# A fixed order for all four engines in the first expert layer of batch 0, and an earlier end of the weight decoding inside attention

## The chip, the cores and the metric

The kernel runs on one core of one Trainium2 chip. The metric is the device time of one execution in microseconds (us). A time of "before" or "after" is the median of three runs. TensorE is called PE, ScalarE ACT, VectorE DVE, GpSimd POOL, SyncE SP; SP only issues DMAs here.

## What is computed

Three layers follow each other. Clustered attention (2 batches, 8 heads, 768 tokens, head size 64) gives x; the first expert layer is a plain two-matrix network on 1536 tokens; a second layer routes each token to two of eight experts.

```python
attn_out = _attn_ref(q, k, v, centroids)            # softmax over keys of the same cluster
x = attn_out.transpose(0, 2, 1, 3).reshape(B * S, H * D)
h = x @ w_in                                        # 1536x512 @ 512x2048
g = h * (1.0 / (1.0 + np.exp(-1.702 * h)))
y = g @ w_out                                       # 1536x2048 @ 2048x512
return _moe2_ref(y, w_gate, w_noise, noise, w1, w2) # top 2 of 8 experts
```

All inputs are float64 or float32; `w_in` and `w_out` come as float64, as pairs of 32-bit words, and have to be turned into float32 on the chip.

## The kernel before

**Stages.** Attention handles one pair of heads of one batch at a time: 8 units (4 of batch 0, then 4 of batch 1) of 12 steps each. Its instructions stand in one list on each engine, sorted by the table `TIMES`, whose entries are in steps; 12 U = 96 is the step at which the last unit would end. The first expert layer then runs on batch 0 (`moe1(0)`) and on batch 1 (`moe1(1)`), and the second layer follows.

**The first expert layer.** The hidden size 2048 is cut into 16 blocks `fb` of 128. Every float32 operand is kept as two parts, a rounded high part and the rest (`wih`, `wil`, `woh`, `wol` for the weights, `xh`, `xl` for x, `gh`, `gl` for g), and a product takes three matmuls. `gemm1(fb)` gives two halves of 384 tokens, 12 matmuls of 384 columns each, in PSUM banks 0 and 1. Each half goes through ACT (`sg`, L736), DVE (`g`, L738), ACT (`gh`, L739) and DVE (`gl`, L740). `gemm2(fb)` adds 18 matmuls of 512 columns into the other six banks. On PE the order is gemm1(0), gemm1(1), gemm2(0), gemm1(2), gemm2(1) and so on; it is fixed by hand. The other engines' order in this layer is chosen by the scheduler at build time. Inside a half the matmuls go `wih*xh, wih*xl, wil*xh` for each quarter of the contraction, so `wil` is wanted by the third matmul.

**Decoding a weight tile.** `decode_part` turns a 128x512 tile of 64-bit words into float32: ACT takes the magnitude (L113) and the sign (L120), POOL clamps (L115), DVE shifts (L116) and ors in the low word (L118), POOL multiplies by the sign (L122). Then `split1` makes the high part on ACT (L717, called hi below) and the low part on POOL (L718, called lo). Each block has two tiles, `wi` and `wo`, so per block: ACT 4 + 2 instructions, POOL 2 clamps, 2 multiplications, 2 lo, DVE 2 shifts and 2 ors, besides sg, g, gh, gl for two halves. For batch 0 this is done for blocks 2 to 15 in the layer itself; blocks 0 and 1 are decoded inside attention, at the steps `w000` to `w114` of the table (block, tile, part). `moe1(1)` reuses the float32 tiles and only splits them.

**Transfers.** SP loads the 64-bit tiles, `si` and `so`, 512 KB each, into two buffers each (`b_stg`). That memory is part of what attention used, so the first of these loads can start only when attention's own tiles there have been read.

**End of attention.** After the last scores a chain of small steps remains for each group of columns: POOL copies (`rb`, L476), PE transposes (L484), DVE copies (L488), POOL adds (L465, L466), multiplies (L492), ACT writes `xh` (L498), POOL `xl` (L505). Their place in the lists is fixed by the table; how they mix with the expert layer's instructions on an engine is the scheduler's choice.

Of the kernel before, what the change touches and what calls it, by code (L numbers as in the profile page):

```python
# [8 lines left out]
F32 = mybir.dt.float32  # L9
# [12 lines left out]
NB = S // 128  # L22
# [22 lines left out]
WARM = (8, 8, 12)  # L45
TAIL = 3
NE = 2
DEC = 5
TIMES = {
# [10 lines left out]
    9.64, "P:xl3": 8.971, "P:xsk": 17.159, "P:xsq": 12.921, "P:ld": 6.496, "P:cc": 8.65, "P:cm0": 10.462,  # L60
    "P:cm1": 10.511, "P:cm2": 10.389, "P:cm3": 9.796, "P:co": 10.569, "P:ct": 11.969, "P:c1": 12.019, "P:ce":
    12.222, "P:cr": 13.092, "P:c2": 14.203, "P:ch": 14.578, "P:ht": 16.263, "P:ho": 22.149, "P:hs": 25.249,
# [6 lines left out]
    7.93, "L:oi": 0.369, "L:or": 7.324, "L:oa": 8.518, "L:ot": 9.79, "L:oc": 10.14, "L:om": 10.5, "L:oh": 11.6, "L:ol":  # L69
# [18 lines left out]
}  # L88
WVE = ()
ORDER = (0, 4, 1, 5, 2, 6, 3, 7)  # L90
# [12 lines left out]
def f(ap):  # L103
    return ap.bitcast(F32)


def decode_part(nc, src, t, dst, part):

    low = src.bitcast(U32).rearrange("p (n t) -> p n t", t=2)[:, :, 0]
    high = src.bitcast(F32).rearrange("p (n t) -> p n t", t=2)[:, :, 1]  # L110
    mag, sgn, bits = t[:, 0], t[:, 1], t[:, 2].bitcast(U32)
    if part == 0:
        nc.scalar.activation(mag, high, AF.Abs, scale=65536.0)  # L113
    elif part == 1:
        nc.gpsimd.tensor_scalar(mag, mag, BIG, TINY, op0=OP.min, op1=OP.max)  # L115
        nc.vector.tensor_scalar(bits, mag.bitcast(U32), 3, 0x7FFFFFFF, op0=OP.logical_shift_left, op1=OP.bitwise_and)  # L116
    elif part == 2:
        nc.vector.scalar_tensor_tensor(bits, low, 29, bits, op0=OP.logical_shift_right, op1=OP.bitwise_or)  # L118
    elif part == 3:
        nc.scalar.activation(sgn, high, AF.Sign)  # L120
    else:
        nc.gpsimd.tensor_mul(dst, f(bits), sgn)  # L122
# [483 lines left out]
class Moe:  # L606
# [87 lines left out]
        nc.sync.dma_start(wo, self.w_out[fb * 128:(fb + 1) * 128])  # L694
        self.st1[fb] = (wi.rearrange("p k f -> p (k f)"), wo)

    def decode(self, src, dst):
        t = self.dec.tile([128, 3, DM], F32, tag="dec", name="dec")
        for part in range(DEC):
            decode_part(self.nc, src, t, dst, part)  # L700

    def split1(self, b, fb):
        nc = self.nc
        if b == 0:
            if fb < NE:
                wi, wo = self.raw[2 * fb:2 * fb + 2]
            else:
                si, so = self.st1.pop(fb)
                wi, wo = (self.wA(F32, 2 * fb + i, f"w{'io'[i]}{fb}") for i in range(2))
                self.decode(si, wi)  # L710
                self.decode(so, wo)
            self.W1.append((wi, wo))
        out = []
        for nm, src in zip(("wi", "wo"), self.W1[fb]):
            hi = self.wr.tile([128, DM], F32R, tag=nm + "h", name=f"{nm}h{fb}")
            lo = self.wr.tile([128, DM], F32R, tag=nm + "l", name=f"{nm}l{fb}")
            nc.scalar.activation(hi, src, AF.Copy)  # L717
            (nc.vector if b else nc.gpsimd).tensor_sub(lo, src, f(hi))  # L718
            out += [hi, lo]
        v = lambda t: t.rearrange("p (k f) -> p k f", k=KB)  # L720
        return v(out[0]), v(out[1]), out[2], out[3]

    def gemm1(self, b, fb):
        nc = self.nc
# [666 lines left out]
@with_exitstack  # L1391
def kernel(ctx, tc, q, k, v, centroids, moe_w_in, moe_w_out,
                                                         w_gate, w_noise, noise, w1, w2, out):
    nc = tc.nc
    pool = lambda c, name, bufs, **kw: c.enter_context(tc.tile_pool(name=name, bufs=bufs, reuse_waits="tile", **kw))
    const = pool(ctx, "const", 1)
    x1 = pool(ctx, "x1", 1, side="right")
    dram = ctx.enter_context(tc.tile_pool(name="dram", bufs=1, space=bass.MemoryType.DRAM))
    xs = dram.tile([E * REG, ROW], F32, name="xs")
    tab = dram.tile([ROUNDS * E, 4], F32, name="tab")  # L1400
    ident = const.tile([128, 128], F32, name="ident")
    make_identity(nc, ident)
    identb = const.tile([128, 128], BF16, name="identb")
    nc.vector.tensor_copy(identb, ident)
    ab = pool(ctx, "a_ab", 1)
    x0ctx = ExitStack()
    x0 = pool(x0ctx, "x0", 1, side="right")
    xh = [p.tile([128, NP, S], F32R, tag=f"xh{b}", name=f"xh{b}") for b, p in enumerate((x0, x1))]
    xl = [p.tile([128, NP, S], F32R, tag=f"xl{b}", name=f"xl{b}") for b, p in enumerate((x0, x1))]
    moe = Moe(tc, const, (moe_w_in, moe_w_out, w_gate, w_noise, noise, w1, w2), ident, xh, xl, xs, tab, out)  # L1410
    moe.x1 = x1
    with ExitStack() as actx:
        a = Attention(tc, actx, const, ab, q, k, v, centroids, (moe_w_in, moe_w_out), ident, identb, xh, xl)
        a.hooks = {3 + 2 * i: [lambda i=i: moe.init_piece(i)] for i in range(44)}
        a.hooks[1] = [moe.consts]
        a.run()
    moe.ab, moe.raw, moe.wg = ab, a.raw, a.g("raw", 0)
    moe.open_all(ctx)
    bctx, b0ctx = ExitStack(), ExitStack()
    moe.open1(bctx, b0ctx)  # L1420
    with tc.high_priority(PRI):
        for fb in range(NE):
            moe.S[0, fb] = moe.split1(0, fb)
        for fb in range(NE, FB1):
            moe.load1(fb)
    with tc.manual_schedule(engines={mybir.EngineType.PE}):
        acc = moe.moe1(0)
    R0 = [moe.row(0, acc, j) for j in range(NB)]
    b0ctx.close()
    x0ctx.close()  # L1430
    moe.open2(ctx)
    s = {"W": []}
    run = moe.logits0(R0)

    def hook(fb):
        if fb % 2:
            s["W"] += moe.weights_part(0, 0, fb // 2, (w1[0], w2[0]))
        if 1 <= fb <= NB:
# [58 lines left out]
```

## Time and profile before

| | us |
|---|---|
| median of 3 runs (lowest, highest) | 949.79 (948.38, 954.39) |
| the profiled execution | 955.92 |
| its span, first to last instruction | 954.2 |
| PE busy in the span | 886.9 (93%) |
| DVE, ACT, POOL busy | 598.8, 491.8, 359.3 |
| mean granted clock of TensorE | 0.969 of 2.4 GHz |

How to read it: matmuls are pipelined, so the busy time of PE counts overlapping instructions once and doesn't mean that the array is at its peak. An instruction that waits for an engine's shared resource after it has started is counted as busy, so a long duration of a short instruction is itself a reading.

### The profile page before, as it was taken

The numbers are of one execution on the slowest core, as the hardware profiler recorded it, in microseconds if no ns is written. First come the engines' busy times: TensorE is split into PE (matmuls) and PEld (weight loads), VectorE is DVE, ScalarE is ACT, GpSimd is POOL, SyncE is SP. The second block draws the span as 40 slices with busy tenths as digits, with TensorE's granted clock in tenths as the row PEclk, the third lists the DMA queues.
The fourth block names the chain that finished last, engine by engine and source line by source line (L and its number), as shares of the span: only waits on it lengthen the run. The fifth ranks groups of instructions, "written<-read, shape, count | busy, mean of one in ns | idle before, by whom it ended". The sixth has DMA issues, their size and how long they took to land. (4 is left out here: it accounts for less than half of the span.)

```text
span 954.2 us, 14930 instructions
## 1 busy us (share of the span) xinstructions
PE 886.9 (93%) x5277; PEld 813.9 (85%) x5277; DVE 598.8 (63%) x1190; ACT 491.8 (52%) x1021; POOL 359.3 (38%) x398
## 2 busy tenths in 40 slices
PE   6999999999895999999999999979999899999993
PEld 4898989899784988888998979868889899999992
DVE  3889999999875667765447553835663446454231
ACT  2788888888875565555345433414443234332210
POOL 3134443444537776770000501462332233342121
PEclk8899999999998999999999999889999899999997
DMA  7756675676314334312100331264675646562120
GB/s 208 187 139 182 166 202 135 178 191 190 112 34 137 103 119 129 103 35 67 45 23 23 145 97 45 78 232 132 210 206 145 159 123 203 152 189 80 33 65 34
DMA packets 77532, 120.14 MB, mean 126 GB/s; under 512 B 9858, under 2 KB 55939, under 8 KB 76941
## 3 DMA queue, kind: packets, MB, share of 16 engines
q1 hardware_dynamic: 69997, 100.98, 36.9%
q0 software_dynamic: 7456, 18.16, 5.9%
q8 instruction: 43, 0.70, 0.3%
q14 instruction: 36, 0.29, 0.1%
HBM read 72.85 MB, written 23.76 MB: 101 GB/s over the span
## 5 line engine op out<-in xcount | busy, mean ns | idle before, releaser
L426 DVE TENSOR_TENSOR PTl<-ps_pt,PTh 128x384 fp32r<-128x384 f32 x192 | 98.7, 549 | 10.5 <-ACT PTh L421 9.5
L421 ACT ACTIVATE PTh<-ps_pt 128x384 fp32r<-128x384 f32 x192 | 87.6, 495 | 28.9 <-PE ps_pt L411 27.4
L733 PE MATMUL bank<-xh,wih 128*128 128x384 f32 x256 | 89.6, 350 | 11.6 <-ACT wih L717 6.3
L394 DVE TENSOR_REDUCE nm<-ps_s 128x1 f32<-128x768 f32 x96 | 91.2, 950 | 12.7 <-PE ps_s L389 12.3
L733 PE MATMUL bank<-xh,wil 128*128 128x384 f32 x256 | 89.1, 348 | 5.5 <-POOL wil L718 5.5
L411 PE MATMUL ps_pt<-ident,P 128*128 128x128 f32 x576 | 88.2, 277 | 3.9 <-DVE PTl L426 3.4
L402 ACT ACTIVATE P<-ps_s,nm 128x768 f32<-128x768 f32 x96 | 87.3, 910 | 4.7 <-DVE nm L394 4.5
L733 PE MATMUL bank<-xl,wih 128*128 128x384 f32 x256 | 87.9, 343 | 0.0
L1259 ACT ACTIVATE hh<-bank 128x240 fp32r<-128x240 f32 (+6 forms) x80 | 35.2, 446 | 99.8 <-PE bank L1251 83.5
L1251 PE MATMUL bank<-xT,wB 128*128 128x240 f32 (+3 forms) x480 | 83.0, 321 | 0.0
L411 PEld LDWEIGHTS ps_pt<-ident,P 128*128 128x128 f32 x576 | 68.3, 141 | 14.3 <-DVE PTl L426 11.5
L1251 PEld LDWEIGHTS bank<-xT,wB 128*128 128x128 f32 x480 | 77.9, 193 | 2.4
L1260 DVE SCALAR_TENSOR_TENSOR hl<-bank,hh 128x240 fp32r<-128x240 f32 (+6 forms) x80 | 40.3, 506 | 57.5 <-ACT hh L1259 56.8
L748 PE MATMUL bank<-woh,gh 128*128 128x512 f32 x192 | 76.3, 397 | 0.0
L748 PE MATMUL bank<-wol,gh 128*128 128x512 f32 x192 | 75.0, 391 | 0.0
L1056 POOL TENSOR_TENSOR wA<-stg,wA 128x512 fp32r<-128x512 f32 x16 | 20.7, 1294 | 142.8 <-DVE wol L718 69.8
L748 PE MATMUL bank<-woh,gl 128*128 128x512 f32 x192 | 70.8, 391 | 0.0
L388 PE MATMUL ps_s<-k,q 128*128 128x384 f32 x192 | 70.3, 366 | 0.2 <-ACT P L402 0.2
L389 PE MATMUL ps_s<-k,q 80*128 80x384 f32 x192 | 66.3, 345 | 2.7 <-DMA q<-ohT 2.7
L1289 POOL DMA_INDIRECT out_dram<-Y,idx x31 | 33.0, 1066 | 78.3 <-DVE Y L1288 68.5
L733 PEld LDWEIGHTS bank<-xh,wih 128*128 128x128 f32 x256 | 49.4, 193 | 14.3 <-ACT wih L717 6.7
L733 PEld LDWEIGHTS bank<-xh,wil 128*128 128x128 f32 x256 | 49.2, 192 | 9.6 <-POOL wil L718 9.5
(294 smaller groups left out, 2206.3 us busy)
## 6 DMA issues: line engine op xcount, KB each, us to landing
stg<-in_moe_w_dram SPq DMA_DIRECT2D x64, 512.0 KB
q<-ABq SPq DMA_DIRECT2D x48, 192.0 KB
k<-ABk SPq DMA_DIRECT2D x48, 192.0 KB
si<-in_moe_w_in_dram SPq DMA_DIRECT2D x14, 512.0 KB
so<-in_moe_w_out_dram SPq DMA_DIRECT2D x14, 512.0 KB
xs<-zrow SPq DMA_DIRECT2D x24, 217.7 KB
ld<-in_k_dram SPq DMA_DIRECT2D x8, 384.0 KB
ld<-in_q_dram SPq DMA_DIRECT2D x8, 384.0 KB
```

The source lines that it names most:

```text
L388: self.nc.tensor.matmul(o, self.g("S1", u, "q")[:, h, qs], self.g("S1", u, "k")[:, h, ks], start=True, stop=False)
L389: self.nc.tensor.matmul(o, self.g("S2", u, "q")[:80, h, qs], self.g("S2", u, "k")[:80, h, ks], start=False, stop=True)
L394: self.nc.vector.tensor_reduce(nm, self.g("s", j)[:, :, :384], axis=AX.XY, op=OP.max, negate=True)
L402: self.nc.scalar.activation(P, self.t.pop(("s", j))[:, :, :384], AF.Exp, bias=self.t.pop(("nm", j)), scale=1.0, accum_out=self.g("sums", u ...
L411: self.nc.tensor.transpose(ps[:, k, :], P[:, k * 128:(k + 1) * 128], self.ident)
L421: self.nc.scalar.activation(self.pt_at(j, g, 0), self.g("pt", j, g), AF.Copy)
L426: self.nc.vector.tensor_sub(self.pt_at(j, g, 1), self.t.pop(("pt", j, g)), f(self.pt_at(j, g, 0)))
L733: nc.tensor.matmul(h, w[:, kb, :], x[b][:, kb, sl], start=(kb == 0 and x is self.xh and w is wih), stop=(kb == KB - 1 and w is wil))
L748: nc.tensor.matmul(acc[j], g[:, sl], w, start=(fb == 0 and n == 0), stop=(fb == FB1 - 1 and n == 2))
L1251: self.nc.tensor.matmul(ps, w[:, kb, :], xT[:, kb, x], start=(kb == 0 and i == 0), stop=(kb == KB - 1 and i == 2))
L1259: self.nc.scalar.activation(hh, ps, AF.Relu)
L1260: self.nc.vector.scalar_tensor_tensor(hl, ps, 0.0, f(hh), op0=OP.max, op1=OP.subtract)
```

## The change

Three things are changed. `decode_part` has six parts instead of five (the clamp on POOL and the shift on DVE become parts of their own). In the table the decoding of blocks 0 and 1 inside attention ends at -5.2 steps, counted from step 96, where it ended at +6.41. And `moe1(0)` is replaced by `moe1_first`: the same instructions for blocks 0 to 15, listed for PE, ACT, DVE and POOL by the table `BLK` (us in a block of 8.35 us), and kept in that order on all four engines. Inside a half of gemm1 the eight matmuls with `wih` now come before the four with `wil`. SP's order stays with the scheduler; the splits of blocks 0 and 1 too.

```diff
-DEC = 5
+DEC = 6
-    ... "w000": -24.468, "w001": -22.329, "w002": -21.543, "w003": -19.819, "w004": -15.88, "w010": -14.68,
-    "w011": -13.896, "w012": -11.61, "w013": -11.04, "w014": -10.84, "w100": -10.71, "w101": -10.317, "w102": -7.66,
-    "w103": -6.958, "w104": -4.95, "w110": -4.776, "w111": -1.765, "w112": 1.827, "w113": 3.51, "w114": 6.41,
+    "wl0": -28.231, "wl1": -16.3, "w000": -25.8, "w001": -25.2, "w002": -23.9, "w003": -23.4, "w004": -23.2,
+    "w005": -22.6, "w010": -20.8, "w011": -20.2, "w012": -18.9, "w013": -18.4, "w014": -18.2, "w015": -17.6,
+    "w100": -13.6, "w101": -13.0, "w102": -11.7, "w103": -11.2, "w104": -11.0, "w105": -10.4, "w110": -8.4,
+    "w111": -7.8, "w112": -6.5, "w113": -6.0, "w114": -5.8, "w115": -5.2,
+BLK = {
+    "P": 8.35, "g1": (0.0, 2.09), "sg": (2.1, 4.45), "g": (2.65, 5.0), "gh": (3.3, 6.1), "gl": (4.2, 7.65), "g2": 4.18,
+    "d": ((-2.05, 0.55, 1.25, 3.15, 0.0, 4.21), (1.3, 2.6, 5.55, 6.55, 3.8, 7.66)), "hi": (5.5, 9.0), "lo": (6.15, 9.65),
+}
...
         nc.gpsimd.tensor_scalar(mag, mag, BIG, TINY, op0=OP.min, op1=OP.max)
+    elif part == 2:
         nc.vector.tensor_scalar(bits, mag.bitcast(U32), 3, 0x7FFFFFFF, op0=OP.logical_shift_left, op1=OP.bitwise_and)
-    elif part == 2:
+    elif part == 3:
         nc.vector.scalar_tensor_tensor(bits, low, 29, bits, op0=OP.logical_shift_right, op1=OP.bitwise_or)
...
+    def moe1_first(self):
...
+            terms = [(wih, x, kb) for kb in range(KB) for x in (self.xh, self.xl)]
+            terms += [(wil, self.xh, kb) for kb in range(KB)]
...
+        for fb in range(FB1):
+            o = fb * K["P"]
+            for half in range(2):
+                for nm, fn in (("g1", g1), ("sg", sg), ("g", g), ("gh", gh), ("gl", gl)):
+                    at(o + K[nm][half], fn, fb, half)
+            at(o + K["P"] + K["g2"], g2, fb)
+            if fb >= NE:
+                for i in range(2):
+                    for part in range(DEC):
+                        at(o - K["P"] + K["d"][i][part], dec, fb, i, part)
+                    at(o - K["P"] + K["hi"][i], hi, fb, i)
+                    at(o - K["P"] + K["lo"][i], lo, fb, i)
...
+        with self.tc.manual_schedule(engines=MANUAL - {mybir.EngineType.SP}):
+            for _, _, fn, a in sorted(ev, key=lambda e: e[:2]):
+                fn(*a)
...
-    with tc.manual_schedule(engines={mybir.EngineType.PE}):
-        acc = moe.moe1(0)
+    acc = moe.moe1_first()
```

## Rows read from the trace of the kernel before

**Rows 1.** Stretches: length, busy PE, PEld, DVE, ACT, POOL, clock, DMA share, GB/s.

```profile
301.00:316.00 15.00, 7.24 (x26) 6.67 (x26) 8.70 (x10) 4.83 (x10) 12.64 (x12) 0.66 0.36 105
316.00:440.00 124.00, 120.02 (x587) 105.54 (x586) 86.56 (x110) 71.79 (x135) 82.05 (x75) 1.00 0.33 102
440.00:600.00 160.00, 156.79 (x869) 142.73 (x868) 84.31 (x217) 70.40 (x137) 21.84 (x19) 0.99 0.17 56
```

**Rows 2.** Timeline of PE: start, duration, line, [idle before <-releaser].

```profile
300.63 0.39 PE L748 MATMUL bank<-woh,gl 128*128 128x512 f32 x1
307.30 0.69 PE L733 MATMUL bank<-xh,wih 128*128 128x384 f32 x1 [6.28 <-ACT wih L717]
309.79 0.69 PE L733 MATMUL bank<-xh,wil 128*128 128x384 f32 x1 [1.49 <-POOL wil L718]
315.77 0.39 PE L748 MATMUL bank<-woh,gh 128*128 128x512 f32 x1
319.88 0.34 PE L733 MATMUL bank<-xh,wih 128*128 128x384 f32 x1
328.19 0.34 PE L733 MATMUL bank<-xh,wih 128*128 128x384 f32 x1
...
426.03 0.34 PE L733 MATMUL bank<-xh,wih 128*128 128x384 f32 x1
430.93 0.40 PE L748 MATMUL bank<-woh,gh 128*128 128x512 f32 x1
```

**Rows 3.** Timeline of POOL over one block.

```profile
389.68 1.32 POOL L718 TENSOR_TENSOR wil<-wi,wih 128x512 fp32r<-128x512 f32 x1 [0.24 <-ACT wih L717]
390.97 1.20 POOL L115 TENSOR_SCALAR dec<-dec 128x512 f32<-128x512 f32 x2
392.43 1.29 POOL L718 TENSOR_TENSOR wol<-wo,woh 128x512 fp32r<-128x512 f32 x1 [0.26 <-ACT woh L717]
394.35 1.32 POOL L122 TENSOR_TENSOR wi<-dec 128x512 f32<-128x512 f32 x1 [0.63 <-DVE dec L118]
397.10 1.31 POOL L122 TENSOR_TENSOR wo<-dec 128x512 f32<-128x512 f32 x1 [1.43 <-DVE dec L118]
```

**Rows 4.** Timeline of DVE over the same block.

```profile
392.48 1.79 DVE L118 SCALAR_TENSOR_TENSOR dec<-si,dec 128x512 uint32<-128x512 uint32 x1
394.66 1.29 DVE L116 TENSOR_SCALAR dec<-dec 128x512 uint32<-128x512 uint32 x1
395.87 0.54 DVE L740 TENSOR_TENSOR gl<-g,gh 128x384 fp32r<-128x384 f32 x1
398.08 0.75 DVE L740 TENSOR_TENSOR gl<-g,gh 128x384 fp32r<-128x384 f32 x1 [0.59 <-ACT gh L739]
```

**Rows 5.** Timelines of DVE and POOL elsewhere in the layer; ACT's hi.

```profile
314.39 0.42 DVE L116 TENSOR_SCALAR dec<-dec 128x512 uint32<-128x512 uint32 x1
320.73 0.69 DVE L118 SCALAR_TENSOR_TENSOR dec<-si,dec 128x512 uint32<-128x512 uint32 x1
320.79 1.79 POOL L718 TENSOR_TENSOR wol<-wo,woh 128x512 fp32r<-128x512 f32 x1 [0.37 <-ACT woh L717]
397.95 0.62 ACT L717 ACTIVATE wih<-wi 128x512 fp32r<-128x512 f32 x1
```

**Rows 6.** Timelines of ACT and SP at attention's end.

```profile
289.35 0.87 ACT L736 ACTIVATE sg<-bank 128x384 f32<-128x384 f32 x2
294.45 0.49 ACT L736 ACTIVATE sg<-bank 128x384 f32<-128x384 f32 x1 [2.55 <-PE bank L733]
304.08 0.42 ACT L498 ACTIVATE xh<-Xn 128x256 fp32r<-128x256 f32 x1 [4.65 <-POOL Xn L492]
291.11 0.40 SPq L692 DMA_DIRECT2D si<-in_moe_w_in_dram  x1
```

**Rows 7.** Stretches of attention, columns as in the first group.

```profile
220.00:250.00 30.00, 28.00 (x204) 25.57 (x202) 28.93 (x50) 25.18 (x56) 14.89 (x21) 1.00 0.58 165
250.00:279.00 29.00, 26.42 (x187) 23.59 (x188) 25.16 (x48) 26.24 (x60) 15.46 (x19) 1.00 0.15 50
```

More of the change, by code (lines that the diff above doesn't have):

```diff
@@ L115, in decode_part @@
         nc.gpsimd.tensor_scalar(mag, mag, BIG, TINY, op0=OP.min, op1=OP.max)
+    elif part == 2:
         nc.vector.tensor_scalar(bits, mag.bitcast(U32), 3, 0x7FFFFFFF, op0=OP.logical_shift_left, op1=OP.bitwise_and)
-    elif part == 2:
+    elif part == 3:
         nc.vector.scalar_tensor_tensor(bits, low, 29, bits, op0=OP.logical_shift_right, op1=OP.bitwise_or)
-    elif part == 3:
+    elif part == 4:
         nc.scalar.activation(sgn, high, AF.Sign)
@@ L695, in load1 @@
         self.st1[fb] = (wi.rearrange("p k f -> p (k f)"), wo)
[L697 to L700, printed above, removed]
     def split1(self, b, fb):
@@ L704, in split1 @@
         if b == 0:
[L705 to L712, printed above, removed]
+            self.W1.append(tuple(self.raw[2 * fb:2 * fb + 2]))
         out = []
@@ L741, in gemm1, with at, dec, hi @@
         return fb, gh, gl, woh, wol
+    def moe1_first(self):
+        nc, ev, K = self.nc, [], BLK
+        acc = [self.bank((2 + j,), [128, DM]) for j in range(NB)]
+        t, G = {}, {}
+        def at(time, fn, *a):
+            ev.append((time, len(ev), fn, a))
+        def dec(fb, i, part):
+            if part == 0:
+                t["d", fb, i] = self.dec.tile([128, 3, DM], F32, tag="dec", name="dec")
+                t["w", fb, i] = self.wA(F32, 2 * fb + i, f"w{'io'[i]}{fb}")
+            decode_part(nc, self.st1[fb][i], t["d", fb, i], t["w", fb, i], part)
+        def hi(fb, i):
+            nm = ("wi", "wo")[i]
+            t["h", fb, i] = self.wr.tile([128, DM], F32R, tag=nm + "h", name=f"{nm}h{fb}")
+            nc.scalar.activation(t["h", fb, i], t["w", fb, i], AF.Copy)
+        def lo(fb, i):
+            nm = ("wi", "wo")[i]
+            t["l", fb, i] = self.wr.tile([128, DM], F32R, tag=nm + "l", name=f"{nm}l{fb}")
+            nc.gpsimd.tensor_sub(t["l", fb, i], t["w", fb, i], f(t["h", fb, i]))
+        def g1(fb, half):
+            if half == 0:
+                if fb >= NE:
+                    v = lambda x: x.rearrange("p (k f) -> p k f", k=KB)
+                    self.S[0, fb] = v(t["h", fb, 0]), v(t["l", fb, 0]), None, None
+                G[fb] = (self.gp.tile([128, S], F32R, tag="gh", name=f"gh{fb}"),
+                         self.gp.tile([128, S], F32R, tag="gl", name=f"gl{fb}"))
+            wih, wil = self.S[0, fb][:2]
+            sl = slice(384 * half, 384 * half + 384)
+            h = t["b", fb, half] = self.bank((0, 1), [128, 384])
+            terms = [(wih, x, kb) for kb in range(KB) for x in (self.xh, self.xl)]
+            terms += [(wil, self.xh, kb) for kb in range(KB)]
+            for n, (w, x, kb) in enumerate(terms):
+                nc.tensor.matmul(h, w[:, kb, :], x[0][:, kb, sl], start=(n == 0), stop=(n == len(terms) - 1))
+        def sg(fb, half):
+            t["s", fb, half] = self.gp.tile([128, 384], F32, tag="sg", name="sg")
+            nc.scalar.activation(t["s", fb, half], t["b", fb, half], AF.Sigmoid, scale=1.702)
+        def g(fb, half):
+            t["g", fb, half] = self.gp.tile([128, 384], F32, tag="g", name="g")
+            nc.vector.tensor_mul(t["g", fb, half], t["b", fb, half], t["s", fb, half])
+        def gh(fb, half):
+            nc.scalar.activation(G[fb][0][:, 384 * half:384 * half + 384], t["g", fb, half], AF.Copy)
+        def gl(fb, half):
+            sl = slice(384 * half, 384 * half + 384)
+            nc.vector.tensor_sub(G[fb][1][:, sl], t["g", fb, half], f(G[fb][0][:, sl]))
+        def g2(fb):
+            w = self.S.pop((0, fb))[2:] if fb < NE else (t["h", fb, 1], t["l", fb, 1])
+            self.gemm2(acc, range(NB), fb, *G[fb], *w)
+        for fb in range(FB1):
[4 more added lines that the diff above has]
+            at(o + K["P"] + K["g2"], g2, fb)
+            if fb >= NE:
+                for i in range(2):
[3 more added lines that the diff above has]
+                    at(o - K["P"] + K["lo"][i], lo, fb, i)
+        self.W1 = [(self.raw[2 * fb], self.raw[2 * fb + 1]) for fb in range(NE)]
+        with self.tc.manual_schedule(engines=MANUAL - {mybir.EngineType.SP}):
+            for _, _, fn, a in sorted(ev, key=lambda e: e[:2]):
+                fn(*a)
+        self.W1 += [(t["w", fb, 0], t["w", fb, 1]) for fb in range(NE, FB1)]
+        return acc
```

6 rows, old and new, of the table TIMES are left out of this document.

## Prediction

> **What bounds the kernel now.** I first read the busy time by stretches [rows 1]. From 316 to 440 us, the layer that is changed, PE is busy 120.02 of 124 us at the full clock, and from 440 on 156.79 of 160: PE bounds both, so time that PE wins in the first moves all that follows. Between 301 and 316 it is busy for 7.24 of 15 us at a granted clock of 0.66, so part of that at 1.2 instead of 2.4 GHz.
>
> The timeline of PE says where it waits [rows 2]. gemm2(0) has been issued at 300.86 (the last row's start plus the usual spacing of 0.23). Then PE idles 6.28 us until ACT has made `wih` of block 2, and 1.49 us more for POOL's `wil`. gemm1(2) takes from 307.30 to 315.77, 8.47 us. An undisturbed pair shows what it should be: 8.31 us from 319.88 to 328.19, of which gemm2(1) took 4.11 (315.77 to 319.88), so 4.20 for a gemm1. From block 4 to 15 the pairs take (426.03 - 328.19) / 11 = 8.89 us, and gemm1(15) takes 4.90. Altogether gemm2(14) starts 130.07 us after gemm2(0) ended, where 14 gemm1 and 13 gemm2 need 14 x 4.20 + 13 x 4.11 = 112.2. So 17.9 us is lost: 6.4 idle, 4.3 in gemm1(2), 7.2 in the later blocks. That is the most that can be won here.
>
> Why the later blocks lose is to be seen on POOL and DVE [rows 3, 4]. A block of POOL has 6.44 us of work and gaps of 0.24, 0.26, 0.63 and 1.43: 9.0 us. The gaps are waits for ACT and for DVE's or and shift, and PE waits for `wil` at the end of that loop. DVE's short instructions are long here: an or takes 0.69 alone [rows 5] but 1.79 when it starts 0.05 after POOL's lo (392.43 to 393.72), and it ends at 394.27, 0.55 after the lo does. A shift ends 0.28 after POOL's multiplication (395.67), gl 0.42 after the next one (398.41). The other way round, where DVE's or starts 0.06 before POOL [rows 5], it takes its 0.69 and POOL's lo 1.79, ending 1.17 after the or. So DVE's shift, or and gl and every POOL instruction here exclude each other, and whoever starts first keeps the other out.
>
> **The change, part by part.** *Attention.* The decoding of blocks 0 and 1 keeps its instructions. What moves across the boundary at 250 us, before which DVE has nothing free (28.93 of 30 us [rows 7]), is one or: 0.69 alone, at most 1.79. In the last unit DVE has 3.84 us free and ACT 2.76, which hides the rest of the moved steps and the splits that follow them; without that cover each ACT or DVE step would cost its 0.6 to 0.7. A gain is excluded, since DVE is full. On SP the load for block 1 (`wl1`) goes 1.6 steps forward and is wanted 2.7 steps after it instead of 4.0; if it came late, ACT would wait in the middle of attention, which the upper bound is to cover. I take 0.5 (0 to 1.8). SP issues the first `si` load at 291.11 [rows 6], when attention's own tiles in that memory have been read. The last of them (the sign, part 3 before, 4 now) goes from step 3.51 to -5.8, so the loads of blocks 2 and 3 can be there before they are wanted. They pass attention's last copies on SP's queue, at 0.40 us an issue. It wins nothing by itself, since ACT has other work till 292.
>
> *Start of the pipeline.* The first sigmoid stays at 289.35 [rows 6]: it sits behind attention's last copy on ACT and its table load. From there ACT and DVE alternate through both halves of block 0 (two each of sg, g and gh at about 0.55): ACT is free near 292.7. The magnitude (about 0.65), clamp 0.6 and shift 0.4 bring it to 294.5; the or sits behind g of block 1, whose sigmoid comes at 294.45 [rows 6], and so ends near 296.3; mul 1.31 and hi 0.62 with their handovers end at 298.4. PE wants it at 300.86, which leaves 2.5 us for attention's leftovers on POOL that come between. `wil` follows 1.4 later and is now wanted 8 matmuls later, 1.4 too. I charge 1.0 for what the leftovers take (0 to 2). The 6.4 us of idle and the 4.3 of gemm1(2) go.
>
> *The steady block.* ACT was busy for 71.79 of 124 us [rows 1], 5.2 in 9, and PE needs 8.31. POOL's round is longer: in the order of the table, with "first come keeps it out" and the times after a release from above (a POOL instruction that DVE holds up ends 0.12 sooner after the release than it lasts), mul 1.17 (behind gl), waiting for hi 0.74 (0.62 [rows 5] and two handovers), lo 1.30, gl 0.42, mul 1.17, clamp 0.60, shift 0.48 with its handover, lo 1.17, or 0.64 (its start overlaps the lo's end), clamp 0.48, gl 0.42: 8.59, so 8.6. The second shift and or fit into the wait for hi. Bounds: 8.31, if PE hides it all, and above it rival A's 8.94; to 8.75, midway, I count it as the forecast. The new order of matmuls gives `wil` 1.4 us instead of 0.35, which is already in this. Two blocks run at 8.31 out of the lead at the start.
>
> A rule of the Trainium skill speaks against this change (SBUF — State Buffer, Who interferes with whom): DVE and GpSimd arbitrate for one port pair, "whoever issues first gets the shared pair for the whole instruction", and the other is blocked. Taken strictly, a block would be 6.44 + 2 x (0.42 + 0.69 + 0.54) = 9.74 us by full durations [rows 4, 5], which would make 126.6 of the 111.2 us below; the trace agrees on the lock, but not on that sum, since the blocks of before hold the same instructions in 8.89 [rows 2].
>
> *Sum.* 300.86 + 0.5 + 1.0 = 302.4 for gemm1(2); 2 x 8.31 + 11 x 8.6 = 111.2 to gemm1(15) at 413.6; 4.2 more and gemm2(14) starts at 417.8 instead of 430.93. 13.1 us sooner. The profiled execution took 955.92 us (a span of 954.2 and 1.7 around it): 942.8. That execution lies 6.1 above the median of the runs, so on their scale I predict 949.8 - 13.1 = 936.7.
>
> **The rivals.** *A. The port is the bound.* If at no handover DVE's start overlaps POOL's end, a block is POOL's 6.44 plus twice 0.28 + 0.55 + 0.42: 8.94. For it: a block of before is 8.89 [rows 2], close to it. Against: POOL's lo took 1.17, not 1.29, after DVE's or [rows 5]. 13 blocks are 116.2 instead of 111.2: gain 8.1, 941.7.
>
> *B. The start stays blocked.* A fixed order on ACT puts hi(2) behind attention's last `xh`, which waited for POOL until 304.08 [rows 6]. Then hi(2) ends at 304.08 + 0.42 + 0.62 + 0.1 = 305.2, 2.8 later than in my sum, and PE has idled over 4 us, after which gemm1(2) ran slow: 8.47 - 1.49 - 4.20 = 2.8 more. Gain 7.5, 942.3. Against: POOL loses two instructions of 1.3 us ahead of that step.
>
> *C. The round of POOL gets longer than the one it replaces (slower).* Place: shift, g and or of DVE between the clamp and the multiplication, now in a fixed order in which g waits for PE and ACT. If nothing overlaps any more, the round is 6.44 + 2.50 + both waits for hi, 1.48, + g 0.55 = 11.0. It loses against before from (111.2 + 13.1) / 13 = 9.56 us a block, and by more than 1% from 10.3. At 11.0 it is 18.7 us slower: 968. Against: this order has work on POOL between every clamp and its multiplication, more than the old one had.
>
> *C2. Half of that:* POOL and DVE stay fully apart but the waits for ACT and PE are hidden. Then every handover costs a full duration, 6.44 + 3.30 = 9.74 a block, 126.6 instead of 111.2: 2.3 slower than before, 952.1. Against: the 0.55 and 1.17 above. This is the skill's rule read strictly.
>
> *D. It doesn't do what it says:* the lists mix so that attention's end comes later by what the layer wins, or PE's own order still waits for POOL's `rb`. The price is that of B or a little more, 943 to 948.
>
> **How the numbers follow.** Forecast 0.57, A 0.15, B 0.13, C 0.05, C2 0.04, D 0.06. The forecast's own range is 931.9 (all of the 17.9 won) to 940.6 (8.75, 2 at the start, 1.8 in attention); with A and B and the spread of the runs, 930 to 945 holds about 0.83. About 1% is what a measurement of this kernel tells from no change, that is 940.3: nearly all of the forecast and a third of A and B lie under it, 0.63; slower by over 1% C and a little of D, 0.06; within 1% 0.31.
>
> **What would show it.** In the profile of after: PE's idle before gemm1(2) under 2 us and its rows at 0.34, not 0.5 (else B); starts of gemm1 8.5 to 8.75 apart from block 4 on (8.9: A; over 9.5: C); gl and shift of 0.8 to 1.3 us still, since they still meet POOL; the first `si` load well before 291; the granted clock between 301 and 316 near 1; attention's last scores within 2 us of before. The prediction fails if the scheduler mixes the two lists differently at attention's end than the trace of before suggests, or if the order on DVE closes a loop through PE that I took to have slack.

## The result, and the profile after

| | before | after |
|---|---|---|
| median, us | 952.09 (4 runs, 948.38 to 955.24) | 940.92 (4 runs, 940.08 to 941.60) |
| ratio, 95% interval | | 0.9884 (0.984 to 0.9928) |
| profiled execution, span | 955.92, 954.2 | 941.51, 939.6 |

The change makes the kernel 1.2% faster. One run of all, a tenth of `e2_decode_sooner` below, took 2206.23 us and is left out of its ratio. The columns of all rows are those explained ahead of the prediction; for stretches: length, busy PE, PEld, DVE, ACT, POOL, clock, DMA share, GB/s. First the stretches of after that answer to [rows 1]:

```profile
301.00:316.00 15.00, 13.42 (x65) 11.19 (x64) 10.76 (x11) 7.69 (x15) 14.25 (x13) 1.00 0.31 94
316.00:440.00 124.00, 124.00 (x609) 108.27 (x608) 85.15 (x115) 72.42 (x139) 94.30 (x74) 1.00 0.32 100
440.00:600.00 160.00, 155.76 (x869) 141.01 (x867) 87.96 (x229) 71.04 (x138) 27.61 (x24) 0.99 0.19 60
```

PE's hole between 301 and 316 is nearly closed (13.42 us busy instead of 7.24), at the full clock. In the layer POOL is busy 94.30 us where it was 82.05, with as many instructions (74 and 75): it now stands longer inside instructions that DVE holds up.

Timeline of PE after, answering to [rows 2]: the starts of gemm1(2), of its `wil` matmuls, of the second block, the third, and the last rows of the layer.

```profile
303.22 0.44 PE L777 MATMUL bank<-xh,wih 128*128 128x384 f32 x1 [0.30 <-ACT wih L757]
306.11 0.97 PE L777 MATMUL bank<-xh,wil 128*128 128x384 f32 x4 [1.22 <-POOL wil L762]
313.38 0.44 PE L777 MATMUL bank<-xh,wih 128*128 128x384 f32 x1
322.01 0.44 PE L777 MATMUL bank<-xh,wih 128*128 128x384 f32 x1
...
416.89 0.44 PE L777 MATMUL bank<-xh,wih 128*128 128x384 f32 x1
421.31 0.39 PE L822 MATMUL bank<-woh,gh 128*128 128x512 f32 x1
```

The wait of 6.28 us for `wih` is 0.30. The first block takes 10.16 us (303.22 to 313.38), the second 8.63, and from block 4 to 15 a block takes (416.89 - 322.01) / 11 = 8.63. gemm2(14) starts 9.6 us sooner than before; counted from the 61st exp, the event used below, it is 7.5 (237.3 and 244.8).

Timelines of POOL and of DVE over one block after, answering to [rows 3] and [rows 4]:

```profile
391.02 1.43 POOL L762 TENSOR_TENSOR wil<-wi,wih 128x512 fp32r<-128x512 f32 x1 [0.74 <-ACT wih L757]
392.40 1.64 POOL L130 TENSOR_TENSOR wo<-dec 128x512 f32<-128x512 f32 x1
394.00 0.62 POOL L122 TENSOR_SCALAR dec<-dec 128x512 f32<-128x512 f32 x1
394.79 1.46 POOL L762 TENSOR_TENSOR wol<-wo,woh 128x512 fp32r<-128x512 f32 x1 [0.17 <-ACT woh L757]
396.21 1.11 POOL L122 TENSOR_SCALAR dec<-dec 128x512 f32<-128x512 f32 x1
397.28 1.63 POOL L130 TENSOR_TENSOR wi<-dec 128x512 f32<-128x512 f32 x1
399.65 1.43 POOL L762 TENSOR_TENSOR wil<-wi,wih 128x512 fp32r<-128x512 f32 x1 [0.74 <-ACT wih L757]
```
```profile
391.39 1.48 DVE L792 TENSOR_TENSOR gl<-g,gh 128x384 fp32r<-128x384 f32 x1
394.65 0.43 DVE L124 TENSOR_SCALAR dec<-dec 128x512 uint32<-128x512 uint32 x1 [1.79 <-POOL dec L122]
395.68 0.56 DVE L785 TENSOR_TENSOR g<-bank,sg 128x384 f32<-128x384 f32 x1 [0.60 <-ACT sg L781]
396.16 0.68 DVE L126 SCALAR_TENSOR_TENSOR dec<-si,dec 128x512 uint32<-128x512 uint32 x1
396.84 0.89 DVE L792 TENSOR_TENSOR gl<-g,gh 128x384 fp32r<-128x384 f32 x1
```

POOL's gaps have shrunk from 2.56 us a block [rows 3] to 0.91, while its six instructions have grown from 6.44 to 7.89 together (their ends overlap a little). The rest of its round sits inside instructions: the multiplication at 392.40 ends 1.17 after DVE's gl (392.87), and lasts 1.64; the clamp at 396.21 lasts 1.11 where 0.62 is its own time. gl ends 0.42 after POOL's lo (392.45). The Trainium skill (SBUF — State Buffer, Who interferes with whom) says that a DVE instruction with two inputs in SBUF contends with a GpSimd instruction that reads SBUF, and one with at most one, outside the modes that use both ports, does not. The rows agree: g, one of whose operands is in PSUM, takes 0.56 at 395.68, in the middle of POOL's lo, and gl, with both outside PSUM, is held.

### The profile page after: what moved, and what is told of

Same layout as the page of the kernel before. It is cut to its first block, busy times and chain, and to the rows that moved or that the text cites. A ratio compares the mean times of both kernels' runs of the same rounds, so it can differ in the third digit from the quotient of the medians.

```text
span 939.6 us, 14934 instructions
## 1 busy us (share of the span) xinstructions
PE 887.8 (94%) x5277; PEld 812.0 (86%) x5277; DVE 592.7 (63%) x1190; ACT 489.6 (52%) x1021; POOL 374.8 (40%) x398
## 3 DMA queue, kind: packets, MB, share of 16 engines
HBM read 72.85 MB, written 23.76 MB: 103 GB/s over the span
## 5 line engine op out<-in xcount | busy, mean ns | idle before, releaser
L1126 ACT ACTIVATE wA<-stg 128x512 fp32r<-128x512 f32 x52 | 32.5, 632 | 43.5 <-DMA stg<-in_moe_w_dram 15.6
L454 PE MATMUL ps_o<-PTl,vs 128*128 128x256 f32 x288 | 54.0, 296 | 0.0
L454 PE MATMUL ps_o<-PTh,vs 128*128 128x256 f32 x288 | 53.7, 295 | 0.3 <-ACT T L461 0.2
L1325 PE MATMUL bank<-xT,wA 128*128 128x240 f32 (+3 forms) x300 | 53.2, 328 | 0.0
L1325 PEld LDWEIGHTS bank<-xT,wA 128*128 128x128 f32 x300 | 49.6, 197 | 1.3
```

The costliest lines, as they stand in the source:

```text
L454: self.nc.tensor.matmul(self.g("O", u, qp)[:, h, :], vs[:, h, 2 * i + half].rearrange("p a d -> p (a d)"), PTx[:, kc, :], start=(c == 1 an ...
L1325: self.nc.tensor.matmul(ps, w[:, kb, :], xT[:, kb, x], start=(kb == 0 and i == 0), stop=(kb == KB - 1 and i == 2))
```

## A measure that fits: from attention's 61st exp to gemm1(15)

Executions of one kernel differ by 3 us in attention's first half, so absolute times of two profiles don't compare well. The 61st of ACT's 96 exps (start 183 to 186 us) lies ahead of all that is changed. From its start I count three parts: to the start of the last exp (attention's end), from there to gemm1(2) (start of the pipeline), and from there to gemm1(15) (13 blocks). All are worked out from starts in the timelines. Of the runs below, those given without a ratio are single runs, so for them this measure counts more than the time.

| kernel | to last exp | to gemm1(2) | 13 blocks | sum | block, late in the layer |
|---|---|---|---|---|---|
| before | 91.95 | 29.26 | 118.73 | 239.94 | 8.97 |
| `e1_control` (before again) | 92.21 | 28.85 | 119.35 | 240.41 | 8.97 |
| after | 94.68 | 24.55 | 113.67 | 232.90 | 8.63 |
| `e10_after` (after again) | 93.33 | 22.65 | 113.46 | 229.44 | 8.61 |
| `e2_decode_sooner` | 97.32 | 24.76 | 112.12 | 234.20 | 8.98 |
| `e3_order_alone` | 91.93 | 27.20 | 112.15 | 231.28 | 8.61 |
| `e4_interleaved` | 93.11 | 23.76 | 114.88 | 231.76 | 8.61 |
| `e5_no_clamp` | 93.56 | 22.07 | 109.65 | 225.28 | 8.31 |
| `e6_lo_dve` | 91.76 | 23.32 | 110.14 | 225.22 | 8.31 |
| `e7_clamp_twice` | 94.84 | 26.48 | 119.82 | 241.14 | 9.19 |
| `e8_table_early` | 91.94 | 21.60 | 113.46 | 226.99 | 8.61 |
| `e9_all` | 91.94 | 20.70 | 109.87 | 222.52 | 8.31 |
| `e9_add_dve` | 93.60 | 22.85 | 112.85 | 229.31 | 8.62 |
| `e11_or_twice` | 93.28 | 23.38 | 121.11 | 237.77 | 9.21 |

## The experiments

### The same kernels again: `e1_control`, `e10_after`

No edit.

> The kernel before, unchanged, profiled once more. The two profiles on record differ by 4.4 us behind the changed layer: in the kernel before, ScalarE stood idle for 10.30 us at 622.62 ahead of the handover to expert 1 and TensorE then waited 5.68 us for an `hh`; in the kernel after there is no such stall. Theory one (the stall belongs to the old kernel): the same stall of about 10 us stands here again, and TensorE's gap of 5.7 us with it. Theory two (it is of one execution): TensorE's gap there is 2 to 3 us, the span is about 4 us shorter, and the changed layer's gain alone (about 10 us) is what the medians show.

950.16 us. ACT's timeline ahead of the handover to expert 1, in before, in `e1_control` and in `e10_after`:

```profile
633.29 0.63 ACT L1259 ACTIVATE hh<-bank 128x240 fp32r<-128x240 f32 x2 [10.30 <-remote]
```
```profile
623.54 0.37 ACT L1259 ACTIVATE hh<-bank 128x240 fp32r<-128x240 f32 x1 [2.41 <-DVE tb L1018]
```
```profile
619.53 0.63 ACT L1333 ACTIVATE hh<-bank 128x240 fp32r<-128x240 f32 x2 [10.06 <-remote]
```

Theory two: the stall isn't the old kernel's. It is absent from the control, and stands in a profile of the changed kernel. So the 14.6 us by which the first two spans differ are not all the change's. 2.1 lie ahead of the 61st exp (186.09 and 183.99) and 5.4 behind the start of gemm1(15) (528.1 and 522.8), where executions of one kernel differ by 3 to 4 us as well (524.9 in `e1_control`, 526.8 in `e10_after`). In the measure the gain is 7 to 11 (239.94 or 240.41 against 232.90 or 229.44).

> The kernel after, unchanged, beside the next ones on one chip, as their measure. Every theory: 939 to 942 us, 8.62 us a block from block 4 on.

944.48 us (4 runs), beside 954.72 for before in the same comparison: a ratio of 0.99 (0.9864 to 0.9937). Both kernels are slower here than elsewhere, and all four profiles of this comparison (with `e9_all`, `e9_add_dve` and `e11_or_twice`) show the stall of 10 us. The runs `e9` to `e11` were on one chip, `e1` to `e8` on two others. So the chip may be the reason; that is not shown, since the first profile of before has the stall too, and its chip isn't known.

### The two halves of the change: `e2_decode_sooner`, `e3_order_alone`

`e2_decode_sooner` is before with the six parts and the new times in attention:

```diff
-DEC = 5
+DEC = 6
-    ... "w112": 1.827, "w113": 3.51, "w114": 6.41,
+    ... "w112": -6.5, "w113": -6.0, "w114": -5.8, "w115": -5.2,
...
```

> The kernel before with attention's decoding in six parts and its new times alone; the first expert layer's order is the old one. Theory (the layer's order carries the gain): the last exp comes about 0.6 us later, the layer still takes 8.97 us a block, the loads of the blocks 2 to 15 still start only at 291; what can be won is a part of the 6.28 us that TensorE waits for the first `wih`, at most 2 us: 949 to 953 us, ratio 0.998 to 1.003. Rival (the sooner decoding carries the gain): gemm1(2) starts 4 us sooner than 307.30, and the time is 947 or less.

A ratio of 0.997 (0.9944 to 0.9996) to before; four runs lie at 942.7 to 944.4 and five at 947.7 to 948.4. The profile, of an execution of 942.88, shows what neither theory had: gemm1(2) comes without a wait for `wih`, and six blocks run at 8.31, before the old 8.98 sets in. ACT's timeline tells why: the loads come sooner, and the scheduler puts the decoding of block 2 into attention, in front of one of the last exps.

```profile
277.48 0.68 ACT L114 ACTIVATE dec<-si 128x512 f32<-128x512 f32 x1 [0.97 <-DMA si<-in_moe_w_in_dram]
278.06 0.66 ACT L122 ACTIVATE dec<-si 128x512 f32<-128x512 f32 x1
278.62 0.89 ACT L404 ACTIVATE P<-ps_s,nm 128x768 f32<-128x768 f32 x1
```

Attention is 5.4 us longer than in before (97.32, 91.95). After, which has no such decoding there but nearly the same clock (0.71 and 0.70 from 235 to 245, see below), has 94.68, so some 2.6 are left for the decoding. Behind attention 11.1 are won. Why five runs take 5 us more, a single profile can't say.

`e3_order_alone` is after with the old table in attention, whose five parts call the six:

```diff
+DECA = 5
...
-        decode_part(self.nc, src, self.g("dec", 0), self.raw[2 * i + n], part)
+        for p in ((0,), (1, 2), (3,), (4,), (5,))[part]:
+            decode_part(self.nc, src, self.g("dec", 0), self.raw[2 * i + n], p)
```

> The kernel after with the old table of attention (decoding in five parts, its last part at step 6.41), so only the layer's order is new. Theory: 8.62 us a block from block 4 on, as in the kernel after; the start depends on when ScalarE, VectorE and GpSimd are rid of attention's last decoding. If the sooner decoding matters, gemm1(2) starts 2 to 4 us later than the 303.22 of the kernel after: 943 to 945 us. Rival (attention's decoding was out of the way anyhow, and its six parts only cost): gemm1(2) starts at 303 or sooner, the last exp comes 0.6 us sooner, 940 to 941 us.

939.85 us, a ratio of 0.991 (0.9879 to 0.994): all of the gain within what can be told. The mechanism that I expected is there, PE waits 5.7 us again ahead of gemm1(2):

```profile
303.83 0.69 PE L778 MATMUL bank<-xh,wih 128*128 128x384 f32 x1 [5.72 <-ACT wih L758]
```

But the time that I expected is not. What PE loses at the start POOL uses to get ahead: the first block takes 10.43, then five run at 8.31, and only from block 9 on 8.61. POOL's round, and not PE's start, sets when the layer ends. The sooner decoding is worth 2.7 us at gemm1(2) in after (27.20 to 24.55) and 4.6 in `e10_after` (22.65); 1.5 and 1.3 of it are given back in the blocks, and attention costs 2.7 and 1.4 more. Net it is 1.6 lost and 1.8 won.

### What sets the block: `e4`, `e5`, `e6`, `e7`, `e11`

`e4_interleaved` has the old order of the matmuls.

```diff
-            terms = [(wih, x, kb) for kb in range(KB) for x in (self.xh, self.xl)]
-            terms += [(wil, self.xh, kb) for kb in range(KB)]
+            terms = [t for kb in range(KB) for t in ((wih, self.xh, kb), (wih, self.xl, kb), (wil, self.xh, kb))]
```

> The kernel after with the old order of terms in gemm1 of the changed layer: for each k the three products wih by xh, wih by xl, wil by xh, where the kernel after has all products of wih first and those of wil last. Theory (the ring of GpSimd and VectorE sets the block): the block stays within 8.55 to 8.7 us; TensorE now waits for `wil` at each block's start instead of `wih`. Rival (the late use of `wil` carries the gain, since it gives GpSimd 1.4 us more): the block grows by 0.5 us or more, to 9.1 us or more, and the time by 6 us or more.

940.04 us, and 8.61 us a block. The late use of `wil` does not carry the gain; the late blocks are POOL's with either order. The first block takes 12.50 here instead of 10.16, and the next three 8.31 to 8.32: again what PE loses at the start is made up behind it.

`e5_no_clamp` leaves out the clamp of the `wo` tiles (that part of the decoding is not computed).

```diff
+            if part == 1 and i == 1:
+                return
             decode_part(nc, self.st1[fb][i], t["d", fb, i], t["w", fb, i], part)
```

> The kernel after without GpSimd's clamp of the magnitude in the decoding of `wo` in the changed layer (that part of the computation is left out; 1.2 to 1.8 us of GpSimd a block, nothing of another engine). Theory (ring of GpSimd and VectorE): the block falls from 8.62 to TensorE's own 8.3 us, the time by 4 to 5 us. Rival one (ScalarE or TensorE sets it): 8.6 us still. Rival two (only GpSimd's sum of work counts): GpSimd's idle time grows by the clamp's full length and the block falls under 8.3 only if TensorE's 8.31 was no bound.

938.41 us, and 8.31 us a block: PE's own time, as by the theory. (The clamp's size in these expectations was wrong: it is 0.62 us alone and 1.11 when DVE holds it up.) The time is 2.5 under that of after, less than the 4 to 5 us; in the measure above the kernel is 4.2 us shorter than `e10_after`. Behind gemm1(15) executions differ by 3 us and more (from its start to the end of the span 528.1 in before, 524.9 in `e1_control`), so one time isn't a measure of a few us.

`e6_lo_dve` puts one of the two subtractions of a block on DVE.

```diff
-            nc.gpsimd.tensor_sub(t["l", fb, i], t["w", fb, i], f(t["h", fb, i]))
+            (nc.vector if i else nc.gpsimd).tensor_sub(t["l", fb, i], t["w", fb, i], f(t["h", fb, i]))
```

> The kernel after with the low part of each `wo` (the subtraction of 1.17 to 1.57 us on GpSimd) on VectorE instead, one of two such subtractions a block. Theory (a ring of GpSimd and VectorE, which hold each other up, sets the 8.62 us): GpSimd has 1.2 us less a block, VectorE 0.5 to 0.7 us more, and the block falls to TensorE's own 8.3 us: 14 blocks by 0.3 us make 4 us, so 936 to 938 us, and TensorE's waits for `wih` (5.5 us over 14 blocks) fall under 2 us. Rival one (ScalarE's order sets the block: it makes `wih` and waits for nothing of GpSimd): 8.6 us still, 940 to 942 us. Rival two (VectorE is the tighter one): 8.8 us or more, 943 us or more.

936.17 us, a ratio of 0.9881 (0.9843 to 0.9919), in a comparison whose before was at 948.74; by the ratio alone it isn't told from after (0.9884), but by the block and the measure it is (225.22 against 232.90 and 229.44). A block takes 8.31 us from block 5 on. Where POOL's lo at 394.79 stood, now DVE has it, in 0.69 us, and POOL has gaps of 0.8 again:

```profile
388.08 0.69 DVE L762 TENSOR_TENSOR wol<-wo,woh 128x512 fp32r<-128x512 f32 x1
```
```profile
388.52 0.72 POOL L122 TENSOR_SCALAR dec<-dec 128x512 f32<-128x512 f32 x1 [0.81 <-ACT dec L120]
390.01 1.64 POOL L130 TENSOR_TENSOR wi<-dec 128x512 f32<-128x512 f32 x1 [0.78 <-DVE dec L126]
```

Rivals one and two fall: ACT has the same work as in after, and DVE has 0.69 us more.

`e7_clamp_twice` does the clamp of `wo` twice, `e11_or_twice` DVE's or of `wo` (the same edit with `part == 3`); the second changes nothing in the values.

```diff
             decode_part(nc, self.st1[fb][i], t["d", fb, i], t["w", fb, i], part)
+            if part == 1 and i == 1:
+                decode_part(nc, self.st1[fb][i], t["d", fb, i], t["w", fb, i], part)
```

> The kernel after with GpSimd's clamp of `wo` done twice in a row (the second changes nothing in the values). Theory (ring of GpSimd and VectorE, with no slack left): the block grows by about half to the whole of a clamp's 1.2 us, since a part of it fills GpSimd's idle time: 9.1 to 9.8 us a block, 947 to 957 us. Rival (GpSimd has 30 us of 124 idle in the steady stretch, 2 us a block, and the block is set by ScalarE or TensorE): 8.6 to 8.7 us still, 942 us or less.

> The kernel after with VectorE's joining `or` of `wo` (0.68 us) done twice in a row in each block of the changed layer; the second changes nothing in the values, and GpSimd has no more to do. VectorE is idle for about 2.9 us of each block. Theory (the two engines hold each other up, so that an operation of either costs the ring its own length): 9.1 to 9.3 us a block, as much as the doubled clamp cost on GpSimd (9.19), and 947 to 950 us. Rival (GpSimd's own queue sets the block; VectorE has slack): 8.6 to 8.75 us a block, 943 us or less.

949.16 and 949.58 us; 9.19 and 9.21 us a block. 0.57 more for a clamp of 0.62, 0.59 more for an or of 0.68: an instruction of either engine costs the round nearly its whole length, though DVE is idle for nearly a third of the stretch in after (busy 85.15 of 124 us). How DVE's part gets there is in the timelines of DVE and POOL in `e11_or_twice`:

```profile
394.32 2.39 DVE L126 SCALAR_TENSOR_TENSOR dec<-so,dec 128x512 uint32<-128x512 uint32 x2
```
```profile
394.75 1.42 POOL L764 TENSOR_TENSOR wil<-wi,wih 128x512 fp32r<-128x512 f32 x1 [0.74 <-ACT wih L759]
396.79 1.56 POOL L130 TENSOR_TENSOR wo<-dec 128x512 f32<-128x512 f32 x1 [0.62 <-DVE dec L126]
```

The second or is held by POOL's lo (which ends at 396.17) and ends at 396.71, 0.54 later; only then can POOL multiply, after an idle 0.62. POOL's queue alone would not have felt it, so the round leads through both engines.

### The start: `e8_table_early`, `e9_add_dve`, `e9_all`

`e8_table_early` adds one sigmoid of a 128x1 tile at step 94.4 of attention.

```diff
+    def s_sig(self):
+        z = self.sm.tile([128, 1], F32, tag="sig", name="sig", bufs=1)
+        self.nc.scalar.activation(z, self.ident[:, 0:1], AF.Sigmoid)
...
+        at(12 * U - 1.6, self.s_sig)
```

> The kernel after with one sigmoid of a 128x1 tile ahead of attention's end, so that ScalarE's table load (1.28 us at 288.66, straight in front of the first `sg`) falls where TensorE has other work. Theory (the load is on the chain from attention to the first gemm2): the first `sg` comes 1.2 us sooner, TensorE's idle time ahead of 291.09 falls from 3.1 to about 1.9 us, and all behind it moves up by 1.2 us, more if the clock falls less long: 938 to 940 us. Rival one (what comes next is bound by GpSimd's leftovers of attention, so `wil` of block 2 and not TensorE sets the start): TensorE gains 1.2 us at 291 and waits that much more for `wil` at 306; 940.5 to 941.5 us. Rival two (the load only moves on to another exp's path and is paid twice): 941 to 943 us.

938.43 us, a ratio of 0.9897 (0.9856 to 0.9938), where before was at 948.80; the intervals don't tell it from after. The mechanism is there: ACT's timeline in after, with the load straight in front of sg, and in `e8_table_early`, with the load in a hole; then, in `e8_table_early`, PE's first row behind it and a transpose that follows.

```profile
288.05 0.60 ACT L461 ACTIVATE T<-ps_o 128x512 f32<-128x512 f32 x1 [2.19 <-PE ps_o L454]
288.66 1.28 ACT L781 ACT_TABLE_LOAD   x1
289.95 0.49 ACT L781 ACTIVATE sg<-bank 128x384 f32<-128x384 f32 x1
```
```profile
278.14 1.28 ACT L225 ACT_TABLE_LOAD   x1
...
285.28 0.60 ACT L465 ACTIVATE T<-ps_o 128x512 f32<-128x512 f32 x1 [2.19 <-PE ps_o L458]
285.77 0.49 ACT L786 ACTIVATE sg<-bank 128x384 f32<-128x384 f32 x1
```
```profile
286.90 0.44 PE L782 MATMUL bank<-xh,wih 128*128 128x384 f32 x1 [1.71 <-DVE g L790]
...
292.01 0.44 PE L496 MATMUL ps_r<-ident,rb 128*128 128x128 f32 x2 [0.41 <-POOL rb L488]
```

PE's wait is 1.71 instead of 3.13. The Trainium skill (ScalarE: Activation LUTs, What ACT_TABLE_LOAD costs) gives about 1.28 us for the load and some 1.4 for a drain with it; the load agrees, but no drain shows (sg starts 0.01 after the load), and 1.42 in all is what it cost here. Each kernel has 7 loads in its trace, so none was paid twice. At gemm1(2) 1.05 of it is left against `e10_after` (22.65 to 21.60): PE now waits 0.41 for POOL's copy `rb`, which it doesn't in `e10_after`, while the wait for `wih` is the same (0.93 and 0.91). Nothing is given back in the blocks (113.46 in both). The other 1.9 against after (24.55) is the clock, below.

`e9_add_dve` moves attention's last two additions from POOL to DVE.

```diff
-        self.nc.gpsimd.tensor_add(Xs[0:64], T[0:64, 0, :], Dm[0:64])
-        self.nc.gpsimd.tensor_add(Xs[64:128], T[64:128, 1, :], Dm[64:128])
+        eng = self.nc.vector if (u, qp) == (len(self.units) - 1, 2) else self.nc.gpsimd
+        eng.tensor_add(Xs[0:64], T[0:64, 0, :], Dm[0:64])
+        eng.tensor_add(Xs[64:128], T[64:128, 1, :], Dm[64:128])
```

> The kernel after with attention's last two additions (1.05 and 0.74 us of GpSimd at 298.64 and 299.77, ahead of the decoding of block 2) on VectorE. Theory (GpSimd's leftovers set the first `wil`, and with it the 1.2 us that TensorE waits at 304.89, and the ring runs without slack from there): TensorE's wait for the first `wil` is gone and gemm1(15) comes 1 to 1.8 us sooner, counted from attention's last exp. Rival (VectorE blocked in its place, or another leftover): the same start within 0.4 us.

943.24 us. The wait for the first `wil` is 0.65, not gone, and counted from the last exp gemm1(15) comes 0.4 sooner than in `e10_after` (135.70, 136.11): nearer to the rival. But that pair isn't equal in the granted clock, which from 286 to 302 was 0.89 here and 1.00 in `e10_after`. At 1.00 in both, `e9_all`, which has this edit, starts gemm1(3) 30.67 us after the last exp, and `e8_table_early`, without it, 31.75: 1.1 sooner, as by the theory. POOL's timeline in after shows what I had missed: two more leftovers of attention stand behind the multiplication and ahead of the first lo, and these stayed.

```profile
298.64 1.05 POOL L473 TENSOR_TENSOR Xs<-T,Dm 64x256 f32<-64x256 f32 x1
299.77 0.74 POOL L474 TENSOR_TENSOR Xs<-T,Dm 64x256 f32<-64x256 f32 x1
300.60 0.62 POOL L122 TENSOR_SCALAR dec<-dec 128x512 f32<-128x512 f32 x1
301.18 1.32 POOL L130 TENSOR_TENSOR raw<-dec 128x512 f32<-128x512 f32 x1
302.45 0.91 POOL L500 TENSOR_TENSOR Xn<-Xn,Xs 128x256 f32<-128x256 f32 x1
303.33 1.19 POOL L513 TENSOR_TENSOR xl<-Xn,xh 128x256 fp32r<-128x256 f32 x1
304.48 1.57 POOL L762 TENSOR_TENSOR wil<-raw,wih 128x512 fp32r<-128x512 f32 x1
```

`e9_all` has the edits of `e6_lo_dve`, `e8_table_early` and `e9_add_dve`.

> Three edits on the kernel after: the low part of `wo` on VectorE (alone 8.31 us a block instead of 8.62), ScalarE's sigmoid table ahead of attention's end (alone TensorE's first wait 1.4 us shorter, and no stretch at the lower clock behind it), and the last two additions of attention's output, 1.05 and 0.74 us of GpSimd at 298.64 and 299.77, on VectorE. Theory (three places on one chain: steady ring, first sg, GpSimd's leftovers ahead of the first `wil`): the gains add up, 4.7 + 2.9 + 0 to 1.5 us in the span from attention's last exp to gemm1(15); 931 to 934 us. Rival (with the layer bound by TensorE, what comes sooner at the start is waited away later, in the next layer's first matmuls): 935 to 937 us, as with the first edit alone.

938.20 us (6 runs) in the comparison in which after is at 944.48 and before at 954.72: a ratio to before of 0.9844 (0.9808 to 0.988), 6.3 us under after. The absolute 931 to 934 was missed, as both other kernels were 4 to 6 us slower there as well. From the last exp to gemm1(15) the gains add up: 130.57 us instead of the 136.11 of `e10_after`, so 5.5 less, where the three edits alone had 2.7, 1.1 and 0.4 (the last understated by the clock). The measure as a whole goes from 229.44 to 222.52, but 1.4 of that is attention's clock (below) and not an edit. It has the lowest ratio of all versions, though its interval overlaps those of after and of `e6_lo_dve`.

## Why the prediction came out as it did

It said 936.7 us, 930 to 945, and faster; 940.92 came. That is just above the forecast's own range (931.9 to 940.6) and close to rival A's 941.7, so the time alone would not choose between them; the block does, below. 2.3 of the 4.2 us are the median of before, which moved from 949.79 to 952.09 with a fourth run. The gain was 11.2 where 13.1 was forecast. In the measure above it forecast 91.95 + 0.5 = 92.45 to the last exp, 23.86 to gemm1(2) (302.4 less 278.54) and 111.2 for the blocks, 227.5. After has 232.90, 5.4 more, and `e10_after` 229.44, 1.9 more: a gain of 7.0 or 10.5 against before where 12.4 was forecast. That the time came as near as 4.2 us is in part luck: single parts of the sum missed by up to 2.7 us, and executions of one kernel differ by 3 us and more. Step by step:

- **The steady block, 8.6.** Right, and for its reason: 8.61 to 8.63 in six profiles with the changed layer, 8.31 once POOL is relieved, 9.2 if either engine gets one instruction more. In the rows of after the terms of the sum come back nearly one by one (the wait for hi 0.74, gl 0.42, mul 1.17, clamp 0.48); the first lo is longer, 1.43 instead of 1.30. Rivals A (8.94), C (11.0) and C2 (9.74) fall: a held instruction needs less than its full time once it is released (0.42, 0.54 and 1.17 in the rows above), and the waits for ACT are short (0.74 and 0.17). Which of the moved instructions shortened the old block of 8.97 was not tried one by one; `e4_interleaved` shows only that PE's order is not it.
- **Two blocks at 8.31 out of the lead.** This step failed. There was no lead: the first blocks took 10.16 and 8.63, 2.2 us more. I had set `wil` 1.4 behind `wih`; POOL had Xn and xl of attention in between (2.1 us), and started lo at 304.48. 0.3 more comes from 8.63 instead of 8.6. Together that is the 2.5 by which 113.67 exceeds 111.2.
- **Start, 1.0 for leftovers.** 24.55 in after and 22.65 in `e10_after`, on either side of 23.86. Both have the same wait of 3.13 us ahead of gemm1(1); what differs is the granted clock behind it. Rival B fell: ACT made hi when POOL's multiplication had ended (302.50), ahead of attention's last `xh`.
- **Attention, 0.5 (0 to 1.8).** 2.7 in after, above the bound, and 1.4 in `e10_after`, but 0 in `e6_lo_dve`, `e8_table_early` and `e9_all`, whose attention is the same up to one tiny sigmoid. The steps were moved at no price by themselves; what I left out is the clock. With the new table PE waits for DVE near 236 and 239, here in after:

```profile
236.33 0.55 PE L419 MATMUL ps_pt<-ident,P 128*128 128x128 f32 x3 [0.83 <-DVE PTl L434]
...
239.47 0.53 PE L359 MATMUL ps_m<-identb,oh 128*64 128x128 bf16 x3 [1.00 <-DVE oh L352]
```

  All kernels with that table have these waits, but not the same clock behind them. In the ten that also have the new order, the part to the last exp goes with the clock from 235 to 245: 91.76 to 91.94 in the three at 1.00, 93.11 to 93.60 in the five at 0.83 or 0.84, 94.68 and 94.84 in the two at 0.71 and 0.70. Stretches in after, `e10_after` and `e8_table_early`, at that place and around the first sg (a clock of 1.00 is 2.4 GHz all the time; below it a part of the stretch was at 1.2):

```profile
235.00:245.00 10.00, 7.83 (x39) 6.64 (x38) 8.57 (x15) 6.31 (x14) 6.01 (x8) 0.71 0.20 55
286.00:302.00 16.00, 12.87 (x59) 11.95 (x59) 7.96 (x19) 8.18 (x15) 8.58 (x12) 0.79 0.14 41
```
```profile
235.00:245.00 10.00, 7.83 (x45) 6.69 (x45) 9.16 (x16) 6.87 (x15) 6.02 (x8) 0.83 0.26 64
286.00:302.00 16.00, 11.62 (x60) 9.63 (x58) 11.03 (x17) 10.56 (x20) 11.66 (x15) 1.00 0.17 44
```
```profile
235.00:245.00 10.00, 7.83 (x59) 6.68 (x57) 9.97 (x18) 7.90 (x18) 6.95 (x10) 1.00 0.22 58
286.00:302.00 16.00, 12.54 (x63) 10.79 (x64) 10.73 (x14) 8.78 (x19) 13.60 (x17) 1.00 0.25 75
```

- **The loads.** Right: SP issues the first `si` at 273.61 instead of 291.11. **Rival D** fell with the result.
- **What carries the gain.** I counted the 6.4 us of idle at the start as a gain of its own, on top of the shorter blocks. `e3_order_alone` shows that this is not so: it keeps 5.72 of them and reaches the same time, as a wait of PE at the start is POOL's lead later. The layer's order carries the gain; the sooner decoding adds nothing that these runs can tell.

## What to carry to other kernels

Where an engine's loop is longer than TensorE's, a wait of TensorE ahead of the loop need be no loss of its own, because the loop gets ahead meanwhile (in `e3_order_alone` five blocks at 8.31 us); what pays is an instruction less in the loop, here one subtraction moved from GpSimd to VectorE (8.63 to 8.31 us a block). Where GpSimd and VectorE work on the same tiles, count both engines' instructions in one round, with the times that remain after a release, and list all leftovers of the stage before that share the queue. Compare profiles from a common event ahead of the change, not by absolute time.

## What was not expected of the hardware

After the same waits, the granted clock was 0.71, 0.83 and 1.00 in three executions of the same stretch (235 to 245, PE busy 7.83 us in each), and attention was 2.7, 1.4 and 0 us longer with it than in before; after the same 3.13 us without a matmul it was 0.79 and 1.00 (286 to 302) in two executions of the same kernel. With the old table the stretches from 220 to 280 were at 1.00 in all three profiles, although TensorE pauses there too; the timeline of PE in before:

```profile
260.33 0.62 PE L446 MATMUL ps_o<-PTh,vs 128*128 128x256 f32 x3 [0.94 <-ACT T L453]
...
262.85 1.01 PE L411 MATMUL ps_pt<-ident,P 128*128 128x128 f32 x6 [0.83 <-DVE PTl L426]
```

So an edit that makes TensorE pause can cost time in some executions only, and not every such pause costs any; what decides it is open. The 10 us in which ACT waited for something outside the core (in before, and in the four profiles of one comparison, in no other profile) stays unexplained.
